# Keys cut as three chunks of 128 and a shared rest, in attention followed by a leaky-ReLU pair of matrix products

## The chip, the cores and the metric

The kernel runs on one core of one Trainium2 chip. The core has five engines that run side by side, each with its own queue of instructions worked off in order: TensorE (PE: matrix products, with results into the PSUM memory; PEld is its loading of the stationary operand), VectorE (DVE), ScalarE (ACT), GpSimd (POOL) and SyncE (SP, which here only issues DMAs). The metric is the device time of one execution in microseconds (us); less is better.

## The reference: what is computed

```python
# q, k, v: (8, 12, 448, 64) float32; w_in: (768, 2048); w_out: (2048, 768)
scores = q @ k.T / sqrt(64)
attn = softmax(scores)                       # along the 448 keys
x = (attn @ v).transpose(0, 2, 1, 3).reshape(3584, 768)
h = x @ w_in
out = maximum(0.01 * h, h) @ w_out           # (3584, 768) float32
```

There are 8 batches of 12 heads, 448 tokens and 64 values per head. The attention's output, 3584 tokens by 768, goes through two products with a leaky ReLU between them.

## The kernel before, in words

**Units.** Two heads of one batch are a unit; there are NU = 48 units, HP = 6 of them per batch. q, k and v of a unit are loaded as float32 and turned to bf16 with 112 partitions (SC = 112, NSC = 4): partition p holds the tokens 4p to 4p+3, so that "chunk" c is made of the tokens 4p+c. Loads of two units at once are issued by POOL (`load_soft`, L137), three by SP at the start (`load_one`, L149). POOL also makes the contiguous copies that the transposes take (`cast`, L162): q and k into `qkb`, v into one of four tiles `v0` to `v3` whose 65th column is 1, so that the product with v also gives the sum of the exponentials.

**Attention of one unit.** `transposes` (L248, on PE with a copy out of PSUM by DVE, for units 0 to 14) or `dma_transposes` (L240, a transposing DMA issued by SP, for units 15 to 47) puts q and k of both heads into `qkT`: 128 partitions (64 for each head), 448 columns of q and 448 of k. `scores` (L267) multiplies one chunk of 112 keys with all 448 queries. It is two matmuls, one for each head, each contracting over 64 partitions, one on the upper and one on the lower half of the array; below they are called a pair. `expo` (L279) is the exponential of a pair on ACT, 112 partitions by 896 values. `rows` (L785; `pv`, L283, for the first units) multiplies the exponentials with v: 2 heads, 4 query chunks and 4 key chunks, 32 matmuls of 65 columns; DVE then takes the reciprocal of the sum and scales. `x_transposes` (L303) turns the unit's rows into columns of `xT`, mostly by a transposing DMA from SP.

**Slots.** Scores and rows write into three PSUM slots of two banks, taken in turn (`next_slot`, L69). A slot is free again when ACT (scores) or DVE (rows) has read it.

**Order of work.** Units 0 to 5 come first, one after another (`first`, L694). Then the two products start for the first tokens (`head`, L616, and `neck`, L635), and after that in seven stages of up to 512 tokens: `hidden(i)` (L445) is the product with w_in, `second(i)` (L933) that with w_out. Both save a product of blocks in eight by sums made on DVE (`mix_x`, `mix_h` and the like). The attention of later units is placed between their matmuls. `burst` (L814) emits three chunks of scores in a row, so four bursts make three units; there are 55 of them after the first six units and the first three chunks of unit 6. `place` (L877) decides between two groups of matmuls whether a burst, a unit's rows or a unit's PE transposes go there. It uses constants: what each costs PE, and when its slots will be free. `early`, `goals` and `plan` say how many bursts each part has to hold.

**Feeding.** `advance` (L763) and `feed` (L853) emit the loads, the casts and the transposing DMAs for later units. POOL's cast of v for unit u overwrites the tile of unit u-4, so POOL waits there for the rows of unit u-4 on PE. SP works off, in one order, the transposing DMAs of qkT and xT and the stores of the output; three output tiles are in use.

Of the kernel before, what the change touches and what calls it, by code (L numbers as in the profile page):

```python
# [9 lines left out]
F32 = mybir.dt.float32  # L10
# [6 lines left out]
def kernel(  # L17
# [33 lines left out]
    cast_pool = ctx.enter_context(tc.tile_pool(name="cast", bufs=3))  # L51
# [29 lines left out]
    v_sb = [v_pool.tile([SC, 2, NSC, D + 1], BF16, name=f"v{i}") for i in range(NV)]  # L81

    NE = 3
    EL = 2 * NSC * S
    e_sb = [exp_pool.tile([SC, EL + P - SC], BF16, name=f"e{i}") for i in range(NE)]
# [3 lines left out]
    QL = 2 * S  # L89
    qkT = [qk_pool.tile([P, QL + P - SC], BF16, name=f"qkT{i}") for i in range(NQ)]  # L90
# [26 lines left out]
    qk_sb = {}  # L117
# [4 lines left out]
    for t in (w_in_mix, w_mix):  # L122
        t = t.rearrange("p x k n -> p (x k n)")
        for j in range(9):
            rooms.append(t[:SC, ts(j, 4 * NSC * D)].bitcast(F32).rearrange("p (h so d) -> p h so d", h=2, so=NSC))

    def room(x):

        return rooms.pop(0) if rooms else ld_pool.tile([SC, 2, NSC, D], F32, name="f" + "qkv"[x])

    def half(t, i=None):

        t = t.rearrange("p h so d -> p (h so d)").bitcast(BF16)
        t = t.rearrange("p (u h so d) -> p u h so d", u=2, h=2, so=NSC)
        return t if i is None else t[:, i]

    def load_soft(u, n, which):  # L137
        b, hp = divmod(u, HP)
        for x in which:
            t = room(x)  # L140
            nc.gpsimd.dma_start(
                out=half(t)[:, :n].rearrange("p u h so d -> p (u h) (so d)"),
                in_=(q, k, v)[x][b, 2 * hp:2 * hp + 2 * n].rearrange(
                    "h (p so) d -> p h (so d)", so=NSC),
            )
            for i in range(n):
                raw.setdefault(u + i, {})[x] = half(t, i)

    def load_one(u, x, queue):  # L149
        b, hp = divmod(u, HP)  # L150
        t = room(x)
        queue.dma_start(
            out=t.rearrange("p h so d -> p h (so d)"),
            in_=(q, k, v)[x][b, 2 * hp:2 * hp + 2].rearrange("h (p so) d -> p h (so d)", so=NSC),
        )
# [6 lines left out]
    def cast(u, parts=(0, 1, 2), by=nc.gpsimd.tensor_copy):  # L162
        if u >= NU:
            return
        for x in parts:
            f = raw[u].pop(x)
            if x < 2 and u not in qk_sb:
                qk_sb[u] = cast_pool.tile([SC, 2, NSC, 2, D], BF16, name="qkb")
            if x < 2:
                by(qk_sb[u][:, x].rearrange("p so h d -> p h so d"), f)  # L170
            else:
                by(v_sb[u % NV][:, :, :, :D], f)  # L172
# [14 lines left out]
    load_one(1, 1, nc.sync)  # L187
    ident = const_pool.tile([P, P], BF16)
# [27 lines left out]
    warm_up(7)  # L216
    for t in v_sb:
        nc.vector.memset(t[:, :, :, D:], 1.0)
    for t in e_sb:
        nc.vector.memset(t[:, EL:], 0.0)  # L220
    for t in qkT:
        nc.vector.memset(t[:, QL:], 0.0)
# [6 lines left out]
    cast(0, (1,), both)  # L229
# [10 lines left out]
    def dma_transposes(u):  # L240
        if NPE <= u < NU:
            turn(qkT[u % NQ][:, :QL], qk_sb[u].rearrange("p i so h d -> p (i so h d)"))

    def turn_tile(bank):
        bank = next_bank() if bank is None else bank
        return bank.bitcast(BF16)[:, :2 * S].rearrange("p (i s) -> p i s", i=2)

    def transposes(u, bank=None):  # L248
        if u >= min(NPE, NU):
            return  # L250
        for parts in ((1,), (0,)) if u == 0 else ((0, 1),):
            tr = turn_tile(bank)
            for i in parts:
                for so in range(NSC):
                    nc.tensor.transpose(  # L255
                        tr[:, i, ts(so, SC)], qk_sb[u][:, i, so], ident[:SC, :SC]
                    )
            if u == 0 and parts == (0,):
                stay_warm(5)
            at = slice(parts[0], parts[-1] + 1)  # L260
            (nc.scalar.copy if u == 0 and parts == (1,) else nc.vector.tensor_copy)(  # L261
                qkT[u % NQ][:, :QL].rearrange("p (i s) -> p i s", i=2)[:, at], tr[:, at]
            )
# [3 lines left out]
    def scores(u, c):  # L267
# [3 lines left out]
        for j in range(2):  # L271
# [756 lines left out]
```

## Time and profile before

| | |
|---|---|
| median of 3 runs | 386.55 us (386.29 to 387.0) |
| profiled execution, its time | 386.18 us |
| its span in the trace | 384.4 us |
| PE busy | 376.4 us (98%), granted clock 1.00 |
| ACT busy | 264.8 us (69%) |
| DVE busy | 233.7 us (61%) |
| POOL busy | 141.3 us (37%) |

A row of the timeline gives the start in us, the duration of the merged run in us, the engine, the line of the kernel, the operation, what it writes and reads, how many instructions are merged (x6) and, in brackets, idle time before it and what ended that. Matmuls are pipelined, so the duration of a run contains the drain of its last matmul; what a run costs is the distance from its start to the start of the next run on PE. L542 and L607 are the product with w_out, L470, L353 and L648 that with w_in, L272 scores, L794 and L291 the product with v, L255 the transposes of q and k, L318 those of x, and L281 the exponential.

### The profile page before, as it was taken

What the parts mean: (1) busy time and instruction counts of PE and PEld (TensorE: products, weight loads), DVE (VectorE), ACT (ScalarE), POOL (GpSimd) and SP (SyncE); (2) the same over time, 40 slices, a digit from 0 to 9 for tenths busy, and PEclk for the clock granted to TensorE, in tenths of its full rate; (3) what the DMA queues carried; (4) which work ended last, traced back from release to release, by engine and by line L of the source; (5) the groups of instructions that cost most, each with busy time, mean ns of one, the idle gap of its engine ahead of it and who ended that gap; (6) DMA issues with size and microseconds to landing.
All of it is one profiled execution on the core that took longest, in us unless ns stands there. A gap on an engine that the chain in (4) does not pass through costs nothing.

```text
span 384.4 us, 10002 instructions
## 1 busy us (share of the span) xinstructions
PE 376.4 (98%) x4090; PEld 261.1 (68%) x4090; DVE 233.7 (61%) x487; ACT 264.8 (69%) x391; POOL 141.3 (37%) x223
## 2 busy tenths in 40 slices
PE   7899999999999999999999999999999999999996
PEld 3565657756588555886558865688656895668854
DVE  2763846665876645666468574576745665474854
ACT  5998885765868776578765877767776687718700
POOL 7998820865547234620436204353042000000000
PEclk9999999999999999999999999999999999999999
DMA  9999999899999968991599914899129600421023
GB/s 154 200 201 203 179 190 180 102 134 204 154 163 105 131 119 137 198 123 26 102 147 179 145 29 66 179 176 151 29 49 179 142 14 3 108 61 46 3 78 87
DMA packets 93246, 46.86 MB, mean 122 GB/s; under 512 B 51856, under 2 KB 89872, under 8 KB 93200
## 3 DMA queue, kind: packets, MB, share of 16 engines
q0 software_dynamic: 37984, 22.47, 46.1%
q1 hardware_dynamic: 55152, 23.73, 32.1%
q8 instruction: 32, 0.52, 0.6%
q14 instruction: 14, 0.11, 0.1%
q10 hardware_dynamic: 64, 0.02, 0.0%
HBM read 45.61 MB, written 11.01 MB: 147 GB/s over the span
## 4 chain that ended last, share of the span: by engine, by line
PE 94%; DMA 2%; DVE 1%; ACT 1%; issue 1%; POOL 1%; POOLq 0%; ACTq 0%; DVEq 0%
PE g L542 32%; PE g L470 14%; PE sc L470 14%; PE sc L794 11%; PE sc L272 11%; PE g L353 4%; PE g L607 3%; PE g L648 2%; DMA w_in_mix<-in_k_dram 2%; PE g L291 1%; PE g L255 1%; PE sc L353 1%; ACT e L281 1%; PE g L318 1%; ACT h L629 0%
## 5 line engine op out<-in xcount | busy, mean ns | idle before, releaser
L281 ACT ACTIVATE e<-sc 112x896 bf16<-112x896 f32 x192 | 163.1, 919 | 48.6 <-PE sc L272 48.5
L542 PEld LDWEIGHTS <-h 128*128 128x128 bf16 x632 | 57.2, 98 | 44.4 <-issue 12.5
L542 PE MATMUL g<-w_out_sb,h 128*128 128x384 bf16 x416 | 81.0, 327 | 0.0
L459 ACT ACTIVATE h<-c 128x512 bf16<-128x512 f32 (+1 forms) x72 | 43.5, 611 | 26.6 <-DVE c L485 18.0
L470 PEld LDWEIGHTS <-w_in_sb 128*128 128x128 bf16 x576 | 54.2, 98 | 6.1
L170 POOL COPY qkb<-fq 112x512 bf16<-112x512 bf16 x38 | 25.3, 666 | 73.8 <-DMA fq<-in_q_dram 38.9
L794 PEld LDWEIGHTS <-e 112*128 112x128 bf16 x1344 | 48.2, 98 | 4.9 <-ACT e L281 0.7
L172 POOL COPY v<-fv 112x512 bf16<-112x512 bf16 x38 | 24.6, 659 | 71.1 <-PE sc L794 69.4
L272 PE MATMUL sc<-qkT 64*128 64x448 bf16 x384 | 49.5, 356 | 1.3 <-DVE qkT L261 0.9
L794 PE MATMUL sc<-v,e 112*128 112x65 bf16 x1344 | 49.8, 194 | 0.4 <-ACT e L281 0.4
L470 PEld LDWEIGHTS <-w_in_mix 128*128 128x128 bf16 x432 | 41.2, 98 | 4.1
L547 DVE COPY o<-g 128x384 f32<-128x384 f32 x49 | 27.1, 554 | 22.1 <-PE g L542 21.8
L542 PE MATMUL g<-w_mix,h 128*128 128x384 bf16 (+1 forms) x208 | 38.3, 324 | 0.0
L272 PEld LDWEIGHTS <-qkT 64*128 64x128 bf16 x384 | 15.3, 94 | 26.6 <-issue 18.3
L800 DVE RECIPROCAL rec<-sc 112x8 f32<-112x8 f32 x42 | 8.7, 207 | 39.7 <-PE sc L794 23.8
L550 DVE TENSOR_TENSOR o<-o,g 128x384 f32<-128x384 f32 x39 | 21.6, 553 | 17.5 <-PE g L542 15.6
L170 POOL COPY qkb<-fk 112x512 bf16<-112x512 bf16 x38 | 24.9, 654 | 14.4 <-DMA fk<-in_k_dram 14.3
L801 DVE TENSOR_TENSOR x<-sc,rec 112x512 bf16<-112x512 f32 x42 | 29.0, 691 | 1.4
L470 PE MATMUL sc<-xT,w_in_sb 128*128 128x256 bf16 (+1 forms) x216 | 28.5, 268 | 0.0
L470 PE MATMUL g<-xT,w_in_sb 128*128 128x256 bf16 (+1 forms) x216 | 28.5, 268 | 0.0
L542 PE MATMUL g<-w_mix,hmix 128*128 128x384 bf16 x104 | 20.1, 327 | 0.0
L470 PE MATMUL sc<-x_mix,w_in_mix 128*128 128x256 bf16 (+1 forms) x144 | 19.0, 268 | 0.0
(103 smaller groups left out, 476.8 us busy)
## 6 DMA issues: line engine op xcount, KB each, us to landing
fq<-in_q_dram POOLq DMA_DIRECT2D x19, 224.0 KB, 6.9
fk<-in_k_dram POOLq DMA_DIRECT2D x19, 224.0 KB, 7.5
fv<-in_v_dram POOLq DMA_DIRECT2D x19, 224.0 KB, 6.2
w_in_sb<-in_moe_w_in_dram POOLq DMA_DIRECT2D x4, 768.0 KB, 10.9
w_out_sb<-in_moe_w_out_dram POOLq DMA_DIRECT2D x4, 768.0 KB, 19.3
out_dram<-o SPq DMA_DIRECT2D x7, 336.0 KB, 4.3
out_dram<-o SPq DMA_DIRECT2D x8, 288.0 KB, 3.5
out_dram<-o SPq DMA_DIRECT2D x7, 240.0 KB, 3.8
```

What stands on the lines that cost most here:

```text
L170: by(qk_sb[u][:, x].rearrange("p so h d -> p h so d"), f)
L172: by(v_sb[u % NV][:, :, :, :D], f)
L272: nc.tensor.matmul(ps[:, j, :S], t[j * D:(j + 1) * D, S + c * SC:S + c * SC + P], t[j * D:(j + 1) * D, :S], start=True, stop=True,)
L281: nc.scalar.activation(e[:, :, c, :], sc_t.pop((u, c))[:SC, :, :S], AX.Exp, scale=scale)
L353: nc.tensor.matmul(open_t[m][:, :n], w_in_sb[:, kk, ts(m, P)], xT[:, kk, at:at + n], start=(fresh and kk == kks[0]), stop=(kk == KD - 1),)
L459: nc.scalar.activation(hs[:, m:m + 2, cols], x.rearrange("p (m t) -> p m t", m=2), AX.Prelu, alpha=0.01)
L470: nc.tensor.matmul(ps[:, j * nh:(j + 1) * nh], w[:, kk, ts(j, P)], x[:, kk], start=(first and j == 0 and kk == 0), stop=(kk == KH - 1), sk ...
L542: nc.tensor.matmul(ps[:, cols], x[:, m], w[:, m], start=(first and m == 0), stop=(m == MH - 1), skip_group_check=True,)
L547: by(o[:, at], ps[:, :NW])
L550: nc.vector.tensor_add(o[:, at], o[:, at], ps[:, :NW])
L794: nc.tensor.matmul(ps[:, j, qc, :], e[:, at:at + P], vt[:, j, c, :], start=(c == 0), stop=(c == NSC - 1),)
L801: nc.vector.tensor_mul(x_t[u].rearrange("p q j d -> p j q d"), ps[:SC, :, :, :D], rec.to_broadcast([SC, 2, NSC, D]))
```

## The change

The 448 keys of a head are cut as three chunks of 128 (KC = 3) and a rest of 64. The first 384 keys lie on 128 partitions, three to a partition. The last 64 keys of the unit's first head lie on partitions 0 to 63 and those of the second on 64 to 127 of one further chunk. In it, k is zero where a partition's keys are not the head's own, and v likewise, so one matmul over 128 partitions gives the rest's scores of both heads, and one matmul of 130 columns multiplies their exponentials with v of both heads. The rests of k and v come by DMAs of their own from SP, as float32, for three units at a time. Queries keep their four chunks of 112, padded to 128 with zero rows before the transpose.

```diff
+    KC = S // P
+    v_sb = [v_pool.tile([P, 2 * KC + 2, D + 1], BF16, name=f"v{i}") for i in range(NV)]
+    qkT = [qk_pool.tile([P, 2, NSC, P], BF16, name=f"qkT{i}") for i in range(NQ)]
+    NB = 3
+    qkb = [cast_pool.tile([P, 2, NSC, 2, D], BF16, name=f"qkb{i}") for i in range(NB)]
...
+    def load_tail(g, home=None):
+
+        b, hp = divmod(3 * g, HP)
+        for x in (1, 2):
+            t = ld_pool.tile([P, 3, D], F32, name="t" + "qkv"[x]) if home is None else home[:, 3 * x - 3:3 * x]
+            tails[g, x] = t
+            for j in range(2):
+                nc.sync.dma_start(
+                    out=t[j * D:(j + 1) * D],
+                    in_=(q, k, v)[x][b, 2 * hp + j:2 * hp + 6:2, KC * P:].rearrange("h p d -> p h d"),
+                )
...
+                if x == 1 and (u + i) % 3 == 0 and u > 2:
+                    load_tail((u + i) // 3)
...
+    def cast_tail(u, x, by=nc.gpsimd.tensor_copy):
+
+        t = tails[u // 3, x]
+        for j in range(2):
+            p = slice(j * D, (j + 1) * D)
+            by(qkb[u % NB][p, 1, KC, j] if x == 1 else v_sb[u % NV][p, 2 * KC + j, :D], t[p, u % 3])
...
     warm_up(7)
+    for t in qkb:
+        nc.vector.memset(t[3 * P // 4:, 0], 0.0)
+        nc.vector.memset(t[:, 1, KC], 0.0)
     for t in v_sb:
-        nc.vector.memset(t[:, :, :, D:], 1.0)
+        nc.vector.memset(t[:, 2 * KC:], 0.0)
+        nc.vector.memset(t[:, :2 * KC, D:], 1.0)
+        for j in range(2):
+            nc.vector.memset(t[j * D:(j + 1) * D, 2 * KC + j, D:], 1.0)
...
+    def transpose_tail(u):
+
+        tr = turn_tile(None)[:, :P]
+        nc.tensor.transpose(tr, qkb[u % NB][:, 1, KC].rearrange("p h d -> p (h d)"), ident)
+        nc.vector.tensor_copy(qkT[u % NQ][:, 1, KC], tr)
...
+        for p, j in ((slice(0, D), 0), (slice(D, P), 1)) if c < KC else ((slice(0, P), 0),):
+            nc.tensor.matmul(
+                ps[:, j, :S].rearrange("p (so s) -> p so s", so=NSC), t[p, 1, c], t[p, 0, :, :SC], start=True, stop=True,
+            )
...
+    def weighted(u, qc, ps):
+
+        e, vt = e_sb[u % NE], v_sb[u % NV]
+        nc.tensor.matmul(
+            ps, e[:, EM + qc * SC:EM + qc * SC + P], vt[:, 2 * KC:].rearrange("p j d -> p (j d)"),
+            start=True, stop=False, skip_group_check=True,
+        )
         for j in range(2):
+            for c in range(KC):
+                at = (j * KC + c) * S + qc * SC
+                nc.tensor.matmul(
+                    ps[:, j * (D + 1):(j + 1) * (D + 1)], e[:, at:at + P], vt[:, j * KC + c],
+                    start=False, stop=(c == KC - 1), skip_group_check=True,
+                )
...
         if u == 0:
+            cast_tail(0, 1, fast)
+            transpose_tail(0)
             cast(2, (0, 1), fast)
...
+    def tail():
+        u = owed_t.pop()
+        scores(u, KC)
+        expo(u, KC)
...
-    plan = [9, 8, 8, 8, 8, 5, 0]
+    plan = [6, 6, 6, 6, 6, 4, 0]
...
-                model["now"] = now + 1.08
-                free[id(t)] = now + 2.33
+                model["now"] = now + 1.04
+                free[id(t)] = now + 2.29
+                continue
+            if owed_t and not late and at[0] <= now + 0.05:
+                t, u = slots[0], owed_t[0]
+                tail()
+                model["act"] = max(model["act"], now + 0.45) + 0.43
+                free[id(t)] = model["act"] + 0.15
+                ready[u] = model["act"] + 0.1
+                model["now"] = now + 0.19
                 continue
...
-    early = [1, 2, 4, 6, 7, 9, 11]
+    early = [1, 4, 7, 9, 11]
```

A burst is now the three full chunks of one unit, so there are 41 bursts after the first six units and unit 6; the shared rest of each unit is a separate step (`tail`) in a slot of its own, and the next burst is placed only after it. A unit's rows are 28 matmuls, four of 130 columns and 24 of 65. In unit 0 the rest of k is cast, transposed and copied apart from the other keys, between the transposes of unit 1 and the last scores of unit 0. The tiles of the rests are two for k and two for v, each for three units. SP issues the loads of such a group at the place where POOL's load of k reaches the group's first unit; the load into a tile waits for the casts of the group two before it.

## The prediction

> **What bounds the kernel now.** I read the granted clock first (1.00 throughout), then the page's first two parts, the chain, PE's waits and last PE's timeline. Page and chain:
>
> ```profile
> PE 376.4 (98%) x4090; PEld 261.1 (68%) x4090; DVE 233.7 (61%) x487; ACT 264.8 (69%) x391; POOL 141.3 (37%) x223
> ...
> PE   7899999999999999999999999999999999999996
> ...
> ACT  5998885765868776578765877767776687718700
> ...
> PE 94%; DMA 2%; DVE 1%; ACT 1%; issue 1%; POOL 1%; POOLq 0%; ACTq 0%; DVEq 0%
> ```
>
> PE is the bound, and ACT, which the change relieves most, isn't. PE's waits come to 4.3 us in all, none of them after 60 us; the two largest are in the start:
>
> ```profile
> PE g L255 <- DVE qkb L170: 1.1, 2, 0.6
> PE sc L272 <- DVE qkT L261: 0.9, 3, 0.5
> ```
>
> So from 60 us on, PE time saved is time saved, and a new wait is time lost. What PE's work costs is read from the distances between starts. First a stretch with a burst and rows in the product with w_out, then single 448-column matmuls, then one cycle of the first units:
>
> ```profile
> 228.68 0.49 PE L542 MATMUL g<-w_mix,h 128*128 128x384 bf16 x2
> 229.10 0.74 PE L272 MATMUL sc<-qkT 64*128 64x448 bf16 x6
> 229.77 1.15 PE L542 MATMUL g<-w_out_sb,h 128*128 128x384 bf16 x6
> 230.76 1.19 PE L794 MATMUL sc<-v,e 112*128 112x65 bf16 x32
> 231.78 0.49 PE L542 MATMUL g<-w_out_sb,h 128*128 128x384 bf16 x2
> ...
> 32.50 3.01 PE L353 MATMUL g<-xT,w_in_sb 128*128 128x448 bf16 x15
> 35.44 0.74 PE L272 MATMUL sc<-qkT 64*128 64x448 bf16 x6
> ...
> 14.80 0.55 PE L272 MATMUL sc<-qkT 64*128 64x448 bf16 x4
> 15.29 0.57 PE L255 MATMUL g<-ident,qkb 112*128 112x112 bf16 x8
> 15.69 0.68 PE L291 MATMUL g<-v,e 112*128 112x65 bf16 x16
> 16.57 0.55 PE L272 MATMUL sc<-qkT 64*128 64x448 bf16 x4 [0.21 <-DVE qkT L261]
> ...
> 26.83 0.37 PE L318 MATMUL g<-ident,x 112*128 112x112 bf16 x4
> 27.13 0.36 PE L272 MATMUL sc<-qkT 64*128 64x448 bf16 x2
> 27.43 1.19 PE L291 MATMUL g<-v,e 112*128 112x65 bf16 x32
> ```
>
> A lone pair costs 0.30 us (27.13 to 27.43), two pairs 0.49 (14.80 to 15.29), three 0.67 (229.10 to 229.77). So a pair is 0.19, its two matmuls running side by side, and leaving a group of pairs costs another 0.10. Entering one costs too: the two 384-column matmuls at 228.68 take 0.42 instead of the 0.33 they take at 231.78 (the next run starts at 232.11). **A burst is 3 x 0.19 + 0.20 = 0.77 us, of which 0.20 is paid at its edges.** A full-height 448-column matmul is (2.94 - 0.09) / 15 = 0.19. Rows are 1.02, so 0.032 for a matmul of 65 columns; a 112-column transpose is 0.40 / 8 = 0.050.
>
> **The change, part by part.**
>
> *Scores.* Outside the first part there are 55 bursts at 0.77 = 42.35 us. After: 41 bursts = 31.57, and 41 rests of one 448-column matmul. That uses all 128 rows, as its neighbours do, so its nearest row is 0.19: 7.79. Sum 39.36, so -2.99. If the rest paid edges like a lone pair (0.30), it would cost 4.5 more; that is the far end, and it can't be below 0.19, which is the streaming of 448 columns. The gain is thus not a chunk fewer (the rest takes a pair's time) but 14 fewer pairs of edges.
>
> *Rows.* Before 1.02. After 24 x 0.032 + 4 matmuls of 130 columns. The rows around it: 65 columns 0.032, 112 columns 0.050, 256 columns 0.109 (six in 0.655); on that line 130 columns are 0.057. 0.77 + 0.23 = 1.00, so -0.025 x 42 units = -1.05. Ends: 0.050 for the 130 gives -2.2; 0.083, a 192-column matmul's time (L648, 24 in 1.99 from 69.55), gives +3.3. I take the line, as 112 is the nearest width.
>
> The Trainium skill (TensorE: Matmul & The Clock Gate, Back-to-back issue gap) speaks against this part: for streams in which every matmul loads its own weights it gives about 81 ns at 128 columns. By that the four wide matmuls would take 0.32 and rows 1.09, a loss of 0.07 per unit and some 3 us in all; but it would also make the transposes here slower than the 50 ns that they take, each with its own weights.
>
> *Transposes on PE.* Eight of 128 instead of 112 columns: +0.0067 each; for units 6 to 14 that is 72 x 0.0067 = +0.48. A unit's first copy to `qkT` is 1024 instead of 896 wide: 0.62 us and 0.39 for 448 make 0.69.
>
> *Units 0 to 5.* PE goes round in 3.13 us (14.80, 17.93, 21.07), with scores of the next unit waiting for DVE's copy, which starts when the transposes end. That stretch (15.29 to 16.57, 1.28) gets +0.05 (transposes) and +0.07 (copy); rows beside it save nothing, the other half unit's rows 0.02. So about +0.08 for each of four cycles: +0.3. ACT's shorter rest (some 0.4 us per unit) stays without effect there. If instead ACT set that pace (its exponentials stand back to back from 13.6 to 26.8), 5 x 0.4 = -2.0 would be the end below.
>
> *The start.* DVE gets 14 more memsets, six of them into `qkb`; at 0.04 to 0.27 each (rows of small ones and of the 128x256 one) they end near 3.2 us, ahead of the 3.71 at which DVE's first cast starts once k has landed; at twice that, +0.5. Unit 0's rest stands on PE between the transposes of unit 1 and the last scores: DVE must finish the copy for unit 1 (about 9.8), make two small casts, PE transposes, DVE copies, so PE stands at the new transpose, with the last scores of unit 0 and the first of unit 1 queued behind it and ACT waiting for both: unit 1's move from 9.75 to about 10.5. But next in line is the cast of k of unit 2, which waited for its load until 10.28 in any case. So most of the 0.8 is absorbed, and I count +0.4; 0 and +1.5 (exponentials starting that much later, nothing absorbed) are the ends.
>
> *POOL, SP, DMAs: counted at nothing.* POOL: casts of k and v are a quarter narrower (0.55 to about 0.43), with four small casts more per unit at 0.10 to 0.29 (its small rows): +0.2 to +0.9 per unit. Cover: idle 69.4 us before casts of v alone; in the first 25 us only a lead of 1.3 us (casts of unit 5 end at 20.2, its transposes start at 21.55), so up to +1 if that is used up. SP: 64 more DMAs of 64 partitions x 3 x 256 bytes, 12288 packets; 33 transposing DMAs grow from 112 x 896 to 128 x 1024, by 1.31, so 4.4 us to landing becomes about 5.7. Cover: qkT is filled up to four units ahead. In bytes the loads stay the same.
>
> The 12288 packets more are of 256 bytes. The hardware queue before moved 55152 packets, 430 bytes on average, in 32.1% of 16 engines' span, 36 ns each; at that they are 28 us for each of the 16 engines, 7% of the span, spread over all of it and partly paid back by q0's narrower loads of k and v. The dense stretch is 10 to 50 us; there the lead of POOL's casts is the cover.
>
> The Trainium skill (DMA: Bandwidth & Descriptors, Specifications) asks for at least 512 bytes per transfer and names read-modify-write below that. Our rests fall under it; were each to cost double for that, the DMA engines would have 56 us more instead of 28, and PE still nothing as long as the loads are ahead.
>
> Sum: -2.99 - 1.05 + 0.48 + 0.3 + 0.4 = **-2.9**. The profiled execution took 386.18, 0.37 below the median, so 383.3 to 383.7: **383.5**.
>
> **The rivals.**
>
> *A. PE waits for slots (ends slower).* Each unit now has three meetings, burst, rest and rows, and the burst needs all three slots free after a rest and rows have just used two. `place` decides by constants. For: a rest can be followed by rows that need its exponential, 0.45 + 0.43 us later. Against: 55 bursts and 42 rows by the same method left no wait after 60 us, and ACT gets 0.4 us lighter per unit. Price: 0.07 us per unit over 41 units eats the 2.9; at 0.15, 389.5.
>
> *B. SP is held by the rests' load.* It waits for POOL's cast of v of the group two before; transposing DMAs and stores stand behind it. In the trace of before the k load of units 20 and 21 was issued at 87.52, and POOL cast v of unit 17 only at 94; SP had transposes at 87.13, 90.93 and 92.42 and stores at 89.83. So up to 7 us held, against a lead of one to two units of some 4.5 us there; I'd price it at 2 to 5 us: 386 to 389. At the later groups the same comparison gives 2 us or less.
>
> *C. The start gains.* ACT set the pace there: -2.0 instead of +0.3, 381.2.
>
> *D. The rest pays edges*, as a lone pair does: +4.5, 388.
>
> **How the numbers follow.** The forecast 0.55, with its own range 382 to 385 (rows at -2.2, start at 0 or +1.5); A 0.19, B 0.13, C 0.08, D 0.05. About 0.2% (0.8 us) is what a measurement can tell. Faster: forecast, C and some small cases of A and B, 0.65; same 0.07; slower 0.28. Leaving out one in ten at each end gives 381.7 to 388.5.
>
> **What the profile would show.** Scores in groups of six, 0.67 to the next start, 41 of them; a single 448-column matmul costing 0.19 with no edge; 28 matmuls of rows in 1.00; PE's waits still under 5 us and none after 60; the first scores of unit 1 near 10.5. I'm wrong if PE's waits show exponentials or qkT after 60 us (A, B), if the rest costs 0.3 (D), or if rows cost over 1.05.

## The result, and the profile after

| | kernel before | changed kernel |
|---|---|---|
| median of the runs made side by side | 386.18 us (6 runs, 385.24 to 387.0) | 390.44 us (6 runs, 389.83 to 391.21) |
| ratio, 95% interval | 1 | 1.0112 [1.0091, 1.0134] |
| profiled execution, its span | 386.18 us, 384.4 us | 391.14 us, 389.0 us |

Medians and ratios here and below leave out single executions that took over 1.5% more than the fastest of their kernel (one of e4, three of e11).

The forecast was 383.5 us, faster. The kernel became slower, by 4.3 us, and the time lies outside the range given (381.7 to 388.5).

First the page of the changed kernel, the same lines as were shown of before, with the granted clock:

```profile
PE 375.7 (97%) x3850; PEld 262.6 (68%) x3850; DVE 232.8 (60%) x510; ACT 249.7 (64%) x391; POOL 179.7 (46%) x407
...
PE   7799997999999999999999999999999999999996
...
ACT  5696884666727878278782787827878378608700
...
PEclk9899999999999999999999999999999999999999
...
PE 84%; DMA 6%; ACT 3%; POOL 2%; DVE 2%; issue 1%; SPq 1%; DVEq 0%; POOLq 0%; ACTq 0%
```

PE is busy 0.7 us less than before and ACT 15.1 us less, yet the span is 4.6 us longer. PE's row is lower in the second slice (7 instead of 8; 10 to 19 us) and the seventh (7 instead of 9; 58 to 68 us), POOL has 38 us more work, and transfers take 6% of the chain instead of 2%.

Now PE's timeline where the predicted costs can be read: a burst and a rest in the product with w_in, and a unit's rows.

```profile
64.00 0.22 PE L334 MATMUL sc<-v,e 128*128 128x130 bf16 x1
64.06 0.35 PE L341 MATMUL sc<-v,e 128*128 128x65 bf16 x6
...
65.00 1.30 PE L411 MATMUL g<-xT,w_in_sb 128*128 128x448 bf16 x6
...
71.21 0.74 PE L317 MATMUL sc<-qkT 64*128 64x448 bf16 x6
71.89 1.33 PE L706 MATMUL g<-xT,w_in_sb 128*128 128x192 bf16 x14
73.05 0.35 PE L317 MATMUL sc<-qkT 128*128 128x448 bf16 x1
73.24 1.99 PE L706 MATMUL g<-xT,w_in_sb 128*128 128x192 bf16 x22
```

From start to start, the burst's six matmuls take 0.68, the rest 0.19 with nothing paid at its edges, the rows 1.00. Those are the prices of the prediction. So the work does cost PE what was said; the loss has to lie between the pieces of work. To find it, the two traces are cut at marks that both have: the first matmul with w_in, the first of 192 columns (in `neck`), and the first matmul of `hidden(1)` and of `hidden(5)`.

| stretch | before | after | difference |
|---|---|---|---|
| start: up to the first matmul with w_in | 25.68 | 29.02 | +3.34 |
| head: from there to the first of 192 columns | 37.19 | 40.28 | +3.09 |
| from there to `hidden(1)` | 42.74 | 42.85 | +0.11 |
| stages: `hidden(1)` to `hidden(5)`, 24 units | 196.32 | 193.72 | -2.60 |
| from there to the end | 82.47 | 83.13 | +0.66 |

The first 70 us lose 6.4 us, and the rest of the kernel gains 1.8. PE's waits, the largest of them, say in what:

```profile
PE sc L376 <- DVE x L860: 1.7, 1, 1.7
PE g L307 <- DVE qkb L190: 1.6, 1, 1.6
...
PE g L298 <- POOL qkb L198: 0.8, 2, 0.5
...
PE g L600 <- DVE o L605: 0.5, 1, 0.5
```

They come to 9.0 us (before 4.3). In the head they are 2.7 us (before 0.6), so 2.1 of its 3.1; where the other 1.0 goes, these views don't show. The second of the lines stands in the start. This is DVE and PE there:

```profile
8.81 0.19 DVE L190 CAST qkb<-tk 64x64 bf16<-64x64 f32 x1 [1.48 <-DMA tk<-in_k_dram]
9.73 0.19 DVE L190 CAST qkb<-tk 64x64 bf16<-64x64 f32 x1 [0.72 <-DMA tk<-in_k_dram]
...
11.84 0.23 PE L307 MATMUL g<-ident,qkb 128*128 128x128 bf16 x1 [1.64 <-DVE qkb L190]
...
12.39 1.04 PE L317 MATMUL sc<-qkT 128*128 128x448 bf16 x3 [0.32 <-DVE qkT L308]
```

DVE waits for the rests' loads, which were issued at 2.3 us and are there only at 8.8 and 9.7. Unit 0's rest is cast and transposed behind that, so the scores that follow come at 12.4; unit 1's first scores stood at 9.75 before. A second loss comes right behind this one. In the 3.41 us before 12.17 PE was busy for 1.12 us, and in the 3.41 us after it the clock granted to PE was 0.50 (columns: stretch, its length, then busy time and count of PE, PEld, DVE, ACT and POOL, clock, DMA share, GB/s):

```profile
12.17:15.58 3.41, 3.19 (x25) 1.96 (x26) 2.22 (x9) 2.60 (x4) 2.33 (x9) 0.50 1.43 181
```

Before the change the clock was 1.00 throughout. Half a clock for 3.41 us is at most 1.7 us of the start's 3.3.

Of the waits above, the first and the third are of the head, the last of the sixth stage. The first of them: VectorE may not write x of unit 11 until the transposing DMA of unit 8, which reads the same tile, has landed. It was issued at 55.2 and took 11.9 us:

```profile
67.21 0.69 DVE L860 TENSOR_TENSOR x<-sc,rec 112x512 bf16<-112x512 f32 x1 [1.80 <-DMA xT<-x]
```

Behind both stretches lie POOL and the DMA engines, whose added work the prediction had counted at nothing. Busy time by stretch, first before, then after. The DMA share adds up the time of every packet, so it passes 1 where packets overlap:

```profile
20.00:40.00 20.00, 19.61 (x260) 11.84 (x256) 10.30 (x26) 17.54 (x25) 18.27 (x30) 1.00 1.34 203
40.00:60.00 20.00, 19.48 (x260) 12.00 (x259) 12.02 (x24) 16.15 (x23) 8.60 (x13) 1.00 1.27 180
```

```profile
20.00:40.00 20.00, 18.88 (x257) 12.03 (x258) 10.35 (x28) 15.88 (x22) 18.99 (x43) 1.00 1.39 198
40.00:60.00 20.00, 19.71 (x227) 11.90 (x224) 13.19 (x26) 16.28 (x26) 18.95 (x39) 1.00 1.27 184
```

POOL's lead is gone: from 40 to 60 us it is busy 18.95 us of 20 instead of 8.60, and from 20 to 40 us it had been busy for 18.27 before the change already. And the transfers of the first 70 us, by queue (packets, MB, the time their packets took as a share of 16 engines), before and after:

```profile
q0 software_dynamic: 15712, 11.45, 110.8%
q1 hardware_dynamic: 2160, 1.03, 9.0%
```

```profile
q0 software_dynamic: 15872, 10.67, 104.8%
q1 hardware_dynamic: 7216, 2.15, 21.3%
```

SP's queue takes 12.3% of 70 us more (8.6 us of packet time on each of the 16 engines), POOL's only 6.0% less (4.2 us). That falls in a stretch in which the DMA engines hardly paused before the change: their row on the page of before has a 9 in each of its first seven slices, up to 67 us.

```profile
DMA  9999999899999968991599914899129600421023
```

### The profile page after: what moved, and what is told of

The parts are those of the page before. It is cut to its first block, busy times and chain, and to the rows that moved or that the text cites. A ratio compares the mean times of both kernels' runs of the same rounds, so it can differ in the third digit from the quotient of the medians.

```text
span 389.0 us, 9850 instructions
## 1 busy us (share of the span) xinstructions
PE 375.7 (97%) x3850; PEld 262.6 (68%) x3850; DVE 232.8 (60%) x510; ACT 249.7 (64%) x391; POOL 179.7 (46%) x407
## 3 DMA queue, kind: packets, MB, share of 16 engines
q1 hardware_dynamic: 72752, 27.90, 37.6%
## 4 chain that ended last, share of the span: by engine, by line
PE 84%; DMA 6%; ACT 3%; POOL 2%; DVE 2%; issue 1%; SPq 1%; DVEq 0%; POOLq 0%; ACTq 0%
PE g L600 29%; PE g L528 14%; PE sc L528 14%; PE sc L317 9%; PE sc L341 7%; DMA xT<-x 4%; PE g L665 3%; ACT e L325 2%; PE sc L334 2%; PE g L411 2%; DMA tk<-in_k_dram 2%; PE g L706 1%; PE g L298 1%; PE g L341 1%; POOL qkb L200 0%
## 5 line engine op out<-in xcount | busy, mean ns | idle before, releaser
L325 ACT ACTIVATE e<-sc 128x896 bf16<-128x896 f32 x144 | 123.0, 919 | 32.0 <-PE sc L317 31.9
L600 PE MATMUL g<-w_out_sb,h 128*128 128x384 bf16 x416 | 78.3, 326 | 0.1
L517 ACT ACTIVATE h<-c 128x512 bf16<-128x512 f32 (+1 forms) x72 | 43.6, 612 | 25.0 <-DVE c L543 15.6
L317 PE MATMUL sc<-qkT 64*128 64x448 bf16 (+1 forms) x336 | 55.0, 361 | 1.2 <-DVE qkT L302 0.6
L341 PEld LDWEIGHTS <-e 128*128 128x128 bf16 x1152 | 50.2, 98 | 2.1
L341 PE MATMUL sc<-v,e 128*128 128x65 bf16 x1008 | 46.5, 193 | 0.0
L528 PEld LDWEIGHTS <-w_in_mix 128*128 128x128 bf16 x432 | 41.2, 98 | 4.1
L334 PE MATMUL sc<-v,e 128*128 128x130 bf16 x168 | 37.0, 220 | 0.0
L327 ACT ACTIVATE e<-sc 128x448 bf16<-128x448 f32 x48 | 26.5, 553 | 8.9 <-PE sc L317 6.8
L317 PEld LDWEIGHTS <-qkT 64*128 64x128 bf16 (+1 forms) x336 | 15.4, 95 | 23.1 <-issue 14.8
L540 ACT COPY c<-g 128x512 f32<-128x512 f32 (+1 forms) x12 | 6.8, 569 | 35.5 <-PE g L528 35.5
L200 POOL COPY qkb<-fk 128x384 bf16<-128x384 bf16 x38 | 21.3, 561 | 14.3 <-DMA fk<-in_k_dram 14.3
```

The lines of the kernel that those rows point to most:

```text
L317: nc.tensor.matmul(ps[:, j, :S].rearrange("p (so s) -> p so s", so=NSC), t[p, 1, c], t[p, 0, :, :SC], start=True, stop=True,)
L325: nc.scalar.activation(e[:, :, c, :], ps[:, :, :S], AX.Exp, scale=scale)
L327: nc.scalar.activation(e[:, EM:EL], ps[:, 0, :S], AX.Exp, scale=scale)
L334: nc.tensor.matmul(ps, e[:, EM + qc * SC:EM + qc * SC + P], vt[:, 2 * KC:].rearrange("p j d -> p (j d)"), start=True, stop=False, skip_gro ...
L341: nc.tensor.matmul(ps[:, j * (D + 1):(j + 1) * (D + 1)], e[:, at:at + P], vt[:, j * KC + c], start=False, stop=(c == KC - 1), skip_group_c ...
L517: nc.scalar.activation(hs[:, m:m + 2, cols], x.rearrange("p (m t) -> p m t", m=2), AX.Prelu, alpha=0.01)
```

## The experiments

Each kernel was profiled in one execution; the marks below are of that one. Kernels with the same start differ in its length by up to 3 us (25.1 and 28.1 in e13 and e14), so a difference in the first column means little unless the times agree. These two do the same work up to there; from 14 to 18 us PE's granted clock was 1.00 in e13 and 0.50 in e14. In the stages, the kernels of the old form agree within 0.1 us; those of the new one within 0.6, or they wait 1.3 to 2.6 us for output tiles there and after (e4, e5, e7, e9, e14).

| kernel | median, us | ratio to before | start | head | stages |
|---|---|---|---|---|---|
| before | 386.2 | 1 | 25.7 | 37.2 | 196.3 |
| changed | 390.4 | 1.0112 | 29.0 | 40.3 | 193.7 |
| e1_memsets | 390.7 | 1.0120 [1.0104, 1.0136] | 28.8 | 40.1 | 194.2 |
| e2_rests_early | 395.0 | 1.0231 [1.0197, 1.0264] | 30.9 | 41.2 | 193.7 |
| e3_three_tv | 391.1 | 1.0134 [1.0109, 1.0158] | 28.8 | 40.0 | 193.7 |
| e4_no_small_casts | 392.9 | 1.0179 [1.0159, 1.0199] | 29.4 | 40.0 | 195.4 |
| e5_rests_not_loaded | 389.0 | 1.0066 [1.0041, 1.0091] | 30.2 | 36.4 | 194.7 |
| e6_before_plus_rests | 391.1 | 1.0134 [1.0111, 1.0157] | 30.2 | 37.3 | 196.3 |
| e7_x8_on_pe | 390.8 | 1.0110 [1.0077, 1.0143] | 28.4 | 38.3 | 194.7 |
| e8_start | 390.3 | 1.0113 [1.0088, 1.0137] | 28.0 | 40.5 | 194.0 |
| e9_rests_cast_by_dma | 409.0 | 1.0609 [1.0582, 1.0636] | 39.0 | 47.3 | 194.7 |
| e10_both | 408.5 | 1.0596 [1.0577, 1.0615] | 39.4 | 47.6 | 193.8 |
| e11_first_ten_as_before | 388.3 | 1.0062 [1.0033, 1.0091] | 27.5 | 39.0 | 193.8 |
| e12_first_six_as_before | 390.4 | 1.0100 [1.0067, 1.0134] | 27.6 | 41.7 | 194.0 |
| e13_first_ten_mended | 388.3 | 1.0040 [1.0017, 1.0063] | 25.1 | 39.3 | 193.6 |
| e14_mended_x8_on_pe | 389.1 | 1.0070 [1.0041, 1.0099] | 28.1 | 38.8 | 196.1 |
| e15_before_plus_casts | 389.5 | 1.0071 [1.0041, 1.0101] | 24.6 | 39.0 | 196.4 |
| e16_before_plus_both | 399.0 | 1.0330 [1.0270, 1.0389] | 31.6 | 44.7 | 196.3 |

### The first four: one suspected wait at a time

**e1_memsets.** The memsets of v and of the exponentials move from DVE to POOL.

```diff
-    for t in v_sb:
-        nc.vector.memset(t[:, 2 * KC:], 0.0)
...
+    for t in v_sb:
+        nc.gpsimd.memset(t[:, 2 * KC:], 0.0)
...
     load_w(1)
```

> Edit: the memsets of the v and exponential tiles go from VectorE to GpSimd, ahead of its first load of w_in; VectorE keeps those of qkb. In the changed kernel VectorE's memsets ran to 4.6 us and the first scores came at 6.58 us instead of 5.87. Theory S (the start loses 3.3 us: 0.7 by memsets, 2.6 by the rests that land late) expects first scores near 5.9 and, if that carries through, 0.7 us less than the changed kernel (389.7). Rival: the rests land at 9.7 us or later whatever VectorE does, so unit 1 starts at 12.4 as before and the time stays at 390.4.

The first scores come at 5.87 us, as before the change, instead of 6.58. But the first matmul with w_in moves by 0.2 only and the time not at all. DVE's memsets, which run to 4.7 us instead of the predicted 3.2, aren't the loss: what follows waits for the rests anyway.

**e2_rests_early.** k's rests of units 0 to 2 are loaded ahead of k of unit 1, and unit 0's rest is cast and transposed ahead of unit 1.

```diff
+    load_tail(0, which=(1,))
     load_one(1, 1, nc.sync)
-    load_tail(0)
+    load_tail(0, which=(2,))
...
     transposes(0)
+    cast_tail(0, 1, fast)
     cast(1, (0, 1), fast)
```

> Edit: the load of the k rests of units 0 to 2 is issued ahead of k of unit 1, the rest of unit 0 is cast ahead of unit 1 and transposed ahead of unit 1's transposes. Theory S expects the last scores of unit 0 to move from 12.4 to about 10 us, the clock not to fall between 10 and 18 us (0.77 to 0.80 in the changed kernel), and 1.5 to 2.5 us less: 388 to 389. If instead the loss is all in the later casts of GpSimd (theory P) or in SP being held (theory H), the gain of the start is eaten by transposes that wait for GpSimd at 30 to 60 us, and the time stays within 0.5 us of 390.4.

The first product with v does come 1.2 us earlier (13.7). Then POOL stands still at 16 and 18 us, 1.5 to 2.0 us each, for the rests of units 3 to 5, whose load waited for a cast and landed at 16 to 18. What is gained at one meeting is lost at the next, and more.

**e3_three_tv.** Three tiles instead of two for v's rests, so that SP isn't held by POOL's casts.

```diff
+    tv_pool = ctx.enter_context(tc.tile_pool(name="tv", bufs=3))
...
-            t = ld_pool.tile([P, 3, D], F32, name="t" + "qkv"[x]) if home
+            t = (ld_pool if x == 1 else tv_pool).tile([P, 3, D], F32, name="t" + "qkv"[x]) if home
```

> Edit: three tiles instead of two for the rests of v, so that SP's load into one waits for an older cast. Theory H (SP is held by that load, the transposing DMA of x behind it comes 3.8 us late at 55 us, and VectorE and PE wait 1.7 us at 67) expects that wait to go and 1.7 us less: 388.7. Theories S and P expect no change (within 0.4 us).

SP issues the DMA for x of unit 8 at 52.6 instead of 55.2, and that DMA lands at 66.6 instead of 67.1. It takes 14.0 us instead of 11.9. When SP issues it hardly matters here. That it lands when the DMA engines get to it is the likely reading; e5 below supports it.

**e4_no_small_casts.** POOL's casts of the rests are left out from unit 3 on.

```diff
-            if x and whole:
+            if x and whole and u < 3:
                 cast_tail(u, x, by)
```

> Leaves out: GpSimd's casts of the rests of k and v for units 3 to 47, so their rests aren't computed with their own data; all other work stays, the rests' loads too, and nothing holds SP for these casts any more. Theory P (the small casts, 0.27 us each and four per unit, keep GpSimd busy from 27 to 62 us, and PE's transposes wait for it, 2.2 us) with H (1.7 us) expects 3.9 us less, 386.5; P alone 2.2 less, 388.2; H alone 1.7 less, 388.7, with the waits of transposes on GpSimd left.

The transposes' waits for POOL vanish, as theory P had it, but the time grows. The DMA for x of unit 8 is issued at 50.6 and takes 15.6 us, PE's wait for it grows from 1.7 to 2.3 us, PE's clock is 0.50 from 67.2 to 70.6 us, and a wait of 1.2 us for an output tile turns up at 163 us. So taking POOL's casts away doesn't win the head back (40.0 us). SP, no longer held by them, also issues the loads earlier here, so this run doesn't price the casts by themselves. After these four, the suspect was what the four had in common, the transfers.

### Loads and casts by themselves

**e5_rests_not_loaded.** The changed kernel without the loads of rests from unit 3 on.

```diff
     def load_tail(g, home=None):
 
+        if g:
+            tails[g, 1], tails[g, 2] = tails[0, 1], tails[0, 2]
+            return
         b, hp = divmod(3 * g, HP)
```

> The changed kernel, but only the rests of units 0 to 2 are loaded; the casts of the rests of units 3 to 47 read those again (so the scores and outputs of the units from 3 on are computed from the wrong 64 keys; all instructions outside SP stay). Theory D: the start and the head are bound by the 16 DMA engines, which are 0.99 busy from 3 us to the first matmul of 192 columns; the rests put 12.3% more of 70 us (8.6 us) on them and the smaller fk and fv take 4.2 us off. Without four of the five groups of rests that are loaded by then about 7 us of it goes: the first matmul of 192 columns comes at 65 to 66.5 instead of 69.3, the wait of 1.7 us for x at 67 us goes, and the time is 386.5 to 388. Rival P (GpSimd, late by its 64x64 casts, orders everything): it keeps its casts, so the milestone stays above 68.5 and the time is 390 to 391.5.

The head takes 36.4 us instead of 40.3, less than before the change, with all of POOL's casts still there. The DMA for x of unit 8, issued at 51.4 us, takes 8.9 us instead of 11.9, and DVE's wait for it is gone. So in the changed kernel the head's loss is tied to these loads. The start isn't better, since units 0 and 1 still wait for theirs, 2.2 and 1.3 us in this execution, and PE's clock falls there (0.73 from 10 to 14 us, 0.50 from 14 to 18). The time, 389.0 us, lies between the ranges of the two theories.

**e6_before_plus_rests.** The converse: the kernel before, unchanged in all that it computes, with the loads of the rests added. Nobody waits for them.

```diff
+    def load_tail(g):
+        b, hp = divmod(3 * g, HP)
+        for x in (1, 2):
+            for j in range(2):
+                nc.sync.dma_start(
+                    out=spare[x, g % 2][j * D:(j + 1) * D],
+                    in_=(q, k, v)[x][b, 2 * hp + j:2 * hp + 6:2, 3 * P:].rearrange("h p d -> p h d"),
+                )
...
+                if x == 1 and (u + i) % 3 == 0 and 2 < u < 13:
+                    load_tail((u + i) // 3)
```

> The kernel before, to which only the loads of the rests of units 0 to 14 are added on SP, into memory that nobody reads. Theory D: nothing waits for these loads, but the DMA engines were full up to 64 us already, so 8 us more of packets push back the load of w_in, w_out and the transposing DMAs of x: first matmul of 192 columns at 65 to 68 instead of 62.9, time 388 to 390.5. Rival W: the rests cost only through what waits for them (casts, transposes, the last scores of a unit): nothing changes, 62.9 and 385.3 to 387.

This is the clearest of the runs: 4.8 us slower than the kernel before, for loads that nobody reads. Here SP has them all issued by 22 us, and all of the loss lies in the start (30.2 instead of 25.7). Much of that can be PE's clock:

```profile
11.65:18.48 6.83, 6.28 (x69) 4.02 (x70) 3.57 (x10) 3.30 (x5) 5.29 (x9) 0.50 1.35 187
```

A clock of 0.50 over 6.83 us is at most 3.4 us of the 4.5; in the 3.41 us before, PE was busy for 1.29. The likely order is that these loads delay those of the first units, PE idles, and the clock falls. The profile doesn't part the two costs, and since none of these loads falls in the head, what they cost there is shown by e5 and not by this run. The stages are untouched (196.3). Theory D's mark for the end of the head (65 to 68) holds with 67.5, and the time is 0.6 above its range; rival W falls.

**e15_before_plus_casts.** The other half alone: the kernel before with the small casts on POOL, for units 3 to 14, on data that is always there.

```diff
+            if x and 2 < u < 15:
+                for j in range(2):
+                    p = slice(j * D, (j + 1) * D)
+                    nc.gpsimd.tensor_copy(small[p, 128:128 + D], small[p, :2 * D].bitcast(F32))
```

> The kernel before with four more copies of 64x64 from f32 to bf16 on GpSimd for each of the units 3 to 14, from memory that is always there into memory that nobody reads: the small casts without the loads of the rests. If GpSimd's lateness alone costs (theory P): 12 units by 1.07 us are 12.8 us more on an engine that had 9.5 of 11 us busy from 29 to 40 and 1.4 of 10 from 50 to 60; transposes wait for it from 30 us on, first matmul of 192 columns at 64 to 67, time 387.5 to 390. If it is hidden (theory D): 62.9 to 63.5 and 385.5 to 387.

The casts alone cost 3.3 us in the median (1.6 to 3.9 by the interval). The profiled execution happened to be the shortest of ten (387.14), so it shows only a part, a head of 39.0 instead of 37.2. Its wait:

```profile
PE g L262 <- POOL qkb L172: 1.9, 2, 1.7
```

So neither theory was right by itself: the loads cost without the casts, and the casts without the loads.

**e16_before_plus_both.** Both together, still with nothing computed differently; now the casts read what the loads bring.

```diff
+                    nc.gpsimd.tensor_copy(x_mix.rearrange("p x k n -> p (x k n)")[p, 2048:2048 + D], spare[x, u // 3 % 2][p, u % 3])
```

> The kernel before with both: the rests of units 0 to 14 are loaded on SP, and for units 3 to 14 GpSimd copies them, 64x64 and to bf16, into memory that nobody reads. No score, no product and no transpose differs from the kernel before. If loads and casts are all that the change loses ahead of the second round, this kernel is slower than the changed one by what the changed one gains after it (2.6 us from the second to the sixth round, up to 3.6 with the rest): first matmul of 192 columns at 68 to 70.5, time 392.5 to 395. If the change loses by something else too (its own waits for the rests, the PE transposes of 128 columns, the memsets), first matmul of 192 columns below 68 and 389.5 to 392.

It costs 13.6 us, where the two by themselves cost 4.8 and 3.3. PE waits for POOL eight times:

```profile
PE g L275 <- POOL qkb L185: 8.8, 8, 4.1
...
POOL x_mix L191 <- DMA x_mix<-in_v_dram: 7.0, 4, 4.2
```

POOL works in order: a small cast that waits for a late load (7.0 us for rests of v, 3.6 more for those of k) holds the casts of q, k and v behind it, and POOL's own loads too. That is how the two together cost more than the sum of both. The expectation was too low. Loads and casts of the rests can thus cost more than the 6.4 us. But this isn't a copy of the changed kernel: there POOL waits for no rest in the first 70 us. This kernel has lost 13.4 us by the first matmul of 192 columns; that the changed one loses less because its other casts and loads are smaller (384 instead of 512 columns, 0.50 instead of 0.61 us) is likely and wasn't tested.

### Attempts to keep the gain

**e7_x8_on_pe** turns x of unit 8 on TensorE, **e8_start** is e2 with a tile of their own for the rests of units 3 to 5.

```diff
-    X_PE = (HP + 3, HP + 4, HP + 5)
+    X_PE = (HP + 2, HP + 3, HP + 4, HP + 5)
```

```diff
-    load_tail(1, spare)
+    load_tail(1)
```

> The changed kernel with x of unit 8 turned on TensorE instead of by SP's DMA, which was issued at 55.2 and took 11.9 us. If the landing of that one DMA sets the wait of 1.7 us at 67 us: the wait goes, four transposes of 112x112 (0.3 with their gaps) come, time 389 to 390. If the whole transfer backlog stands behind it, the wait moves to the next thing that is loaded in the head, and the time is 390 to 391.5.

> The changed kernel with the k rests of units 0 to 2 loaded ahead of k of unit 1, the rest of unit 0 cast and transposed ahead of unit 1, and the rests of units 3 to 5 loaded into a tile of their own, so that the load doesn't wait for a cast. Theory S (the start loses 3.3 us because the rests stand in a row behind other work): first product with v at 13.7 as in the second experiment, no wait on GpSimd's cast at 16 to 24 us, first matmul of w_in at 27.6 to 28.2 instead of 29.0, time 389.3 to 390.3. Theory D: the same bytes have to come before the same stage; what is loaded earlier delays q, k and v of units 2 to 5, the first matmul of w_in stays at 28.6 to 29.4 and the time at 390 to 391.5.

e7 wins 2.0 us in the head and 0.6 in the start by its profile, and gives 1 us back on the way to `hidden(1)` and 1.2 in the next stage; PE waits 0.5 and 0.9 us for output tiles there, where the changed kernel doesn't wait for them. e8 has the start that theory S expected (28.0) and no longer holds POOL, which is worth 1.1 us in the profile and can't be told from nothing in the time.

**e9_rests_cast_by_dma** loads the rests through POOL's queue, cast on the way, instead of through SP's; **e10_both** adds e7's edit.

```diff
-                nc.sync.dma_start(
+                (nc.gpsimd if g else nc.sync).dma_start(
```

> The kernel of e8_start with one edit: from the second group on the rests are loaded by GpSimd's queue and cast to bf16 on the way, as q, k and v are, instead of by SP's in f32 (the small casts stay, from bf16). Theory D (the head's loss is transfer time): before, a packet of GpSimd's queue took 68 ns for 604 bytes that it wrote, the rests' 28 ns for about 212; cast on the way they write half of it. If the time goes by bytes written, the groups of the head cost half (3.5 instead of 7 us of all engines), SP is never held, and the stretch from the first matmul of w_in to the first of 192 columns takes 37.5 to 39 us instead of 40.5; with the same start (28.0) that milestone comes at 65.5 to 67 and the time at 387 to 389. Rival T (a packet costs its own time, whatever it writes, and GpSimd's four issues of 0.7 us for three units come on top of a queue that has no gap from 27 to 62 us): the stretch takes 40 to 42 us, time 390 to 392.5.

> The kernel of e9_rests_cast_by_dma, with x of unit 8 turned on TensorE as in e7_x8_on_pe. Theory D: both take load off the same stretch, the first matmul of 192 columns at 64.5 to 66.5, but what e7 won there (2.6 us) was mostly given back in the stages after, so the time is 386.5 to 389. Rival T: no better than e7, 390 to 392.

Both miss even the rival's price by far: 23 us slower than before, all of it by 87 us. POOL's timeline in the start of e9:

```profile
10.12 1.35 POOL L161 DMA_DIRECT2D tk<-in_k_dram  x2 [0.97 <-DMA w_in_mix<-in_k_dram]
12.27 0.63 POOL L161 DMA_DIRECT2D tv<-in_v_dram  x1 [0.81 <-DMA w_in_mix<-in_v_dram]
...
19.87 0.52 POOL L194 COPY qkb<-tk 64x64 bf16<-64x64 bf16 x2 [2.81 <-DMA tk<-in_k_dram]
```

Each of these issues takes POOL 0.62 to 0.68 us and waits for older loads to land, so all casts behind it come late; then the rest itself is awaited for 2.8 us. PE's clock in the next 20 us was 0.71 and 0.78. Whether a cast on the way makes the transfer itself cheaper can't be seen under that.

**e11, e12, e13, e14** are the other way out: units 0 to 9 (in e12, 0 to 5) as in the kernel before, all others as changed. The core of it:

```diff
+    U0 = 10
...
-        for p, j in ((slice(0, D), 0), (slice(D, P), 1)) if c < KC else ((slice(0, P), 0),):
+        for p, j in ((slice(0, D), 0), (slice(D, P), 1)) if c < KC or u < U0 else ((slice(0, P), 0),):
...
+        for j in range(2 if u < U0 else 0):
+            for c in range(NSC):
+                w, at = (e, (j * KC + c) * S + qc * SC) if c < KC else (e_more[u % 2], j * S + qc * SC)
+                nc.tensor.matmul(
+                    ps[:, j * (D + 1):(j + 1) * (D + 1)], w[:SC, at:at + P], vt[:SC, j * NSC + c],
+                    start=(c == 0), stop=(c == NSC - 1),
+                )
```

> The changed kernel from unit 10 on; units 0 to 9 are computed as in the kernel before (four chunks of 112 keys, no rests, no block of zeros), and the v rests have three tiles. No rests are loaded before about 25 us and GpSimd has no small casts before about 44 us. Theory G (the change gains 0.108 us per unit in the steady stages, and loses only where the start and the head are bound by transfers and GpSimd): first scores, first product with v and first matmul of w_in where they were before the change (5.9, 11.7, 25.7), first matmul of 192 columns at 63 to 65 (two or three groups of rests still fall before it), then the steady stages of the changed kernel (193.7 instead of 196.3 from the second to the sixth round): 383 to 385.5, below the kernel before. Rival M (the loss moves along to wherever the rests begin, since the transfers are full until 64 us): first matmul of 192 columns at 66 or later, time 386 to 389.

> The same with units 0 to 5 as before and all others as changed: the start without rests, the head with them. Theory G: first matmul of w_in at 25.7 to 26.5; from there to the first matmul of 192 columns between the 37.2 of the kernel before and the 40.3 of the changed one, since the groups for units 6 to 14 load in the full stretch, so that milestone at 64 to 66.5 and the time at 385 to 387. Rival M: all of the loss follows, 68 or later and 389 to 391.

> The kernel of e11_first_ten_as_before, with 16 columns between the two buffers of the fourth chunk's exponentials. Theory G: the three waits of 0.4 to 1.0 us before the product with v (2.4 in all) go, the first matmul of w_in comes at 25.2 to 26.2 instead of 27.5, the span is 383.4 to 384.8 and the time 385 to 387, level with the kernel before or a little below. Rival M: what comes earlier waits longer for the transfers of the head (x of unit 8), span 385 to 386.5, time 387 to 389.

> The same with x of unit 8 turned on TensorE. Theory G: the wait for x in the head (1.1 us) goes too; in e7_x8_on_pe the head gained 2.6 us by this and most of it was given back before the second round, so 0 to 1.5 us below e13: time 384 to 386.5. Rival M: no gain, 386.5 to 389.

In e11 the new buffer for the fourth chunk's exponentials let a window of 128 columns reach 16 columns into the next unit's, and PE waited for the wrong exponentials:

```profile
PE g L357 <- ACT x_mix L345: 2.4, 3, 1.0
```

e13 takes that away, and its start is that of the kernel before (25.1). e11's expectation that no rests load before 25 us doesn't hold: SP, with nothing to wait for, issues those of units 9 to 14 by 8 us, in e13 too. Its head is still 39.3: the rests of units 10 to 14 are cast there, POOL sets their zeros and ones, the rests of units 15 to 17 load there, and x of unit 8 is again awaited for 1.2 us. The stages take 193.6 us.

This profiled execution is the shortest of twelve, 386.18 us, with the span of the kernel before (384.4): 1.5 us lost up to the first matmul of 192 columns, 2.7 gained in the stages. The median is 388.3 us, 2.2 us less than the changed kernel and still 0.4% more than the kernel before; where the other executions lose 2 us isn't seen. So the truth lies between the two theories: the gain of the stages holds, and part of the loss moves along to where the rests are cast and loaded next. e12 has a head of 41.7 us, with a clock of 0.50 over 3.4 us of it, and e11's fault besides (2.3 us in the start), so its time of 390.4 prices the earlier rests poorly. e14, with x of unit 8 on TensorE, wins nothing: PE waits 2.6 us for output tiles, and its clock was half in the start. No kernel tried here beats the one before.

## Why the prediction was wrong, point by point

- **Scores and rows (-2.99 and -1.05): right.** Worked out for 24 units they are 24 x (2.99 / 41 + 0.025) = 2.35; the four stages between `hidden(1)` and `hidden(5)` gained 2.60. Every kernel that keeps the old form in the stages has 196.3 or 196.4 there, and nine of the fourteen others have 193.6 to 194.2. The rest costs 0.19 without edges; rival D is out.
- **Units 0 to 5 (+0.3): right in size.** From the first product with v to the first matmul with w_in it is 14.08 us (14.01 before), and one cycle 3.18 (3.13), where the terms given (0.05 and 0.07 less 0.02) make 0.10 and not 0.08 a cycle. ACT didn't set the pace; rival C is out. The transposes' +0.48 couldn't be read apart from the waits around them.
- **"The start", +0.4 with ends at 0 and +1.5: failed,** 3.3 in the profile. The working looked at the order of DVE's and PE's work and let the rests be there. They landed 6.5 us and more after their issue, beside everything else that is loaded first. Unit 1's first scores came at about 12.9, not 10.5, and PE, idle meanwhile, had a clock of 0.77 and 0.80 from 10 to 18 us (1.00 before). A fall of the clock had no term in the sum; it can be up to 1.7 of the 3.3. How the rest divides among these waits and the extra transfers stays open: the starts vary too much from one execution to the next.
- **"POOL, SP, DMAs: counted at nothing": failed,** and this is the step that decided. The cover that it named, the lead of POOL's casts, was used up (18.95 us of 20). The packets were estimated at 28 us of each DMA engine and took 23 (32.1% of 384.4 us before, 37.6% of 389.0 after); but the estimate spread them over the whole span, where 8.6 of them fall in the first 70 us, and there on top of packet times that came to 1.27 to 1.34 of all engines already. "The dense stretch is 10 to 50 us" was read too short: the page's DMA row has its 9s up to 67 us. "POOL, up to +1 if that is used up" was a bound for POOL alone. In the changed kernel the head's loss goes when the loads go (e5, 36.4 instead of 40.3). In the kernel before, loads, casts and both together cost 4.8, 3.3 and 13.6 us (e6, e15, e16), so the term was never near nothing; how the changed kernel's 6.4 us divide between the two stays open.
- **Rival A (slots): not seen.** PE's waits for exponentials are 0.3 us in all. After 72 us two waits are left, of 0.5 us each, for an exit of the leaky ReLU in `neck` and for an output tile at 342 us; with the second the last stretch loses 0.66 where the units there should have gained.
- **Rival B (SP held): seen, but without its price.** SP's loads of rests were held by POOL's casts for up to 17.7 us (18.6 to 36.3 us); e3 took away the holds of 4.4 and 2.4 us by casts of v between 37 and 54 us, and the time stayed. Its place was the head, not 87 us.
- **The tests it named worked.** PE's waits "under 5 us and none after 60" were 9.0 us, and 3.1 of them came after 60.

A rule of the skill that the prediction weighed can now be held against a measurement. Counted by size in the trace of the changed kernel, SP's queue moved 5952 packets of 256 bytes up to 70 us in 31 ns each and 512 of 768 bytes in 52 ns each, 0.12 and 0.07 ns per byte. The Trainium skill (DMA: Bandwidth & Descriptors, Specifications) wants at least 512 bytes per transfer for full rate. The direction agrees. The prediction's 36 ns for a packet was a mean over all sizes; the trace of before had packets of the rests' own size to read, 47040 of 256 bytes at 28 ns each, which makes 22 us for 12288 of them and is close to the 23 measured. Doubling the 36 ns was too much. The rests cost because of when they come, and not because each is dear.

## What to carry to other kernels

"Hidden" is a statement about a stretch, not about a kernel: an engine that is busy 37% of the span, or DMA queues at 78%, can be full for the first 60 us, and what is added there can be paid for. Cost each addition against the busiest window that it falls in. Two queues that wait for each other can cost more together than the sum of both, as in e16. And look at the granted clock behind every new wait of PE: in the starts here such a wait could cost its own length and then up to half of the next 3.4 or 6.8 us. When a gain is proved in the steady part and lost at the beginning, a mixed form is worth a try, but part of the loss can follow to the place where the new form begins, as in e13.

## What the runs showed of the hardware beyond that

- A small load isn't a fast one beside others: the rests' 48 KB took 6.5 us from issue to the first landing at the start, and the transposing DMA of unit 8's x 11.9 to 15.6 us in the head, with almost the same landing time whenever it was issued (66.1 to 67.1 us for issues from 50.6 to 55.2, in the changed kernel, e1, e3 and e4). Without the loads of the rests, in e5, it took 8.9 us from 51.4.
- GpSimd pays 0.23 to 0.27 us for a copy of 64 x 64, when one of 128 x 384 takes 0.50: a twelfth of the elements for half the time.
- PE's granted clock was 0.77 from 10 to 14 us, where PE was busy for 2.04 of 4.00 us, still 0.80 in the next 4 us, in which it was busy for 3.95, and 1.00 again from 18 us on. The Trainium skill (TensorE: Matmul & The Clock Gate, What's actually happening) has the clock go to half speed after an idle window of about 3.4 us. These rows are means over 4 us. In windows of 3.41 us the step shows: 0.50 from 12.17 to 15.58 us, after a window in which PE was busy for 1.12 us, so the window before the fall wasn't wholly idle. In all the traces here there are 22 such falls ahead of the kernels' ends, and PE was busy for 0.2 to 2.1 us of the 3.41 before each. It isn't a sure sign: e15 has such a stretch with 1.6 and no fall. The kernel before is close to it, with 2.2 us in its emptiest 3.41. Of 72 executions of it made beside the experiments, 7 have a mean clock of 0.996 or less, and their median is 388.1 us, that of the others 385.7.
